# Attention scores as plain fp32 products over each head's own 64 rows, instead of split one-pass products

## The chip, the cores and the metric

The kernel runs on one core of a Trainium2 chip. The core has five engines that run side by side: TensorE (matrix products, PE in the profile; its weight loads are PEld), VectorE (DVE), ScalarE (ACT), GpSimd (POOL) and SyncE (SP), which here issues all DMA transfers in order. SBUF is the working memory of 128 partitions (rows); PSUM is the memory of 8 banks into which TensorE writes. The metric is device microseconds of one execution, lower is better.

## The reference

Softcapped attention for 4 batches of 12 heads, 448 positions, 64 features a head, followed by a bilinear feed-forward layer over the 1792 tokens of 768 features:

```
scores = cap * tanh((q @ k.T) / sqrt(64) / cap)       # [4, 12, 448, 448]
attn   = exp(scores - max); attn /= sum(attn) + 1e-9
x      = (attn @ v), heads side by side               # [1792, 768]
out    = ((x @ w_a) * (x @ w_b)) @ w_out              # w_a, w_b: [768, 1536], w_out: [1536, 768]
```

q and k are fp32 normal numbers with a spread of about 0.41; cap is 30. The outputs are fp32.

## The kernel before

**Pairs.** Heads are handled two at a time, 24 pairs in all. Each pair has 128 rows in SBUF: head A's 64 features on partitions 0 to 63, head B's on 64 to 127. The number 448 is cut into three chunks of 128 keys and a remainder of 64.

**The steps of a pair.** `load_pair` issues the loads of k, q and v. `prep_pair` brings q and k into the layout [feature, position] and makes the operands of the scores. `scores(pi, 0)` does chunks 0 and 1, `scores(pi, 1)` chunk 2 and the remainder: products into the PSUM tile `psc` (two banks, one for each head; two such tiles in turn), tanh on ScalarE out of `psc` (L270), exp in place (L271). The remainder of both heads shares one bank. GpSimd and VectorE add up the exponentials (L275 to L281, tile `psum`). `attend` multiplies with v (L293, L295, tile `pv`; plain fp32 products, each head in its own half of the columns), `normalize` sums over rows with small products (L308), takes reciprocals (L316), sends them through DRAM to broadcast them (L317, L321), and multiplies (L322). For pairs 0 to 11 the result is split into a high and a low part, `xhi` and `xlo` (L331, L332); for pairs 12 to 23 it goes to DRAM and is loaded later (L326, L337).

**How products are made.** `F32R` is a form of fp32 that TensorE multiplies in one pass with fewer bits. Where full precision is wanted in one-pass products, an operand is split into `hi` (the value cast to F32R) and `lo` (the rest), and a product is hi·hi + lo·hi + hi·lo. An operand of plain type F32 makes a plain fp32 product.

**q and k before.** For pairs 0 to 12, q and k are loaded as [112, 4, 2, 64], transposed by TensorE against the identity (L232, tiles `ptk`, `ptq`, `pt`) into PSUM, and read from there. For pairs 13 to 23 (`BLOCKED`) they are loaded in blocks of 32 features (L206, 128-byte pieces) and transposed by VectorE in 32x32 blocks (L223). Then ScalarE casts q's high part onto the head's own 64 rows of `qhh` (L238), and a copy of it goes onto the other 64 rows (L240 for pairs 0 and 1, a DMA at L242 after that); VectorE casts k's high part onto the own rows of `keys` (L245), and k's low part goes onto the other rows (L247, VectorE or GpSimd); GpSimd keeps the remainder's high parts on the diagonal of `kdiag` (L248); VectorE makes `qlo` (L250). So a product over all 128 rows is (k hi + k lo)·q hi of one head (L263), and one over the own 64 rows adds k hi·q lo (L264). The remainder takes three products over 128 rows (L268 twice, L269).

**Order.** A loop over pairs calls the steps in the order of a string, "PASNFTF" up to pair 12 and "SFANPFTF" after: P prepares the next pair, A and N attend and normalize the one before, S and T are the two halves of the scores, F runs a slice of the feed-forward generator `ffn`. A scheduler then orders each engine's instructions by that priority and by when it expects operands. `load_pair` runs two pairs ahead; q, k and their prepared tiles have two buffers, v three.

**The feed-forward part** is done in two groups of 896 tokens. Group 0 runs in slices between pairs 13 to 23 and finishes after them; group 1 follows. `ffn` makes products over 768 features (L429 to L431, tiles `pha`, `phb`), multiplies the halves (L434 to L438) and calls `ffn_out`, products with w_out (L460 to L462, tile `po`), added up in `acc` (L466). The weights come as 64-bit words and are converted by `ready_w` on ScalarE, VectorE and GpSimd (L389 to L394), written to DRAM for group 1 (L395), and split by `split_w` (L411, L412); the first loads are issued after pair 10's scores.

Of the kernel before, what the change touches and what calls it, by code (L numbers as in the profile page):

```python
# [9 lines left out]
F32 = mybir.dt.float32  # L10
# [11 lines left out]
def wide_cap_path(tc, q, k, v, wd, capt, ident, out):  # L22
    """The whole computation with the softmax's running maximum, for caps that exp alone can't span."""
# [93 lines left out]
def kernel(  # L117
# [30 lines left out]
    MAIN = NC3 * P  # L148
    R = S - MAIN
# [6 lines left out]
    BLOCKED = NPG + 1  # L156
# [21 lines left out]
    def f32(ap):  # L178
        return ap.bitcast(F32)
# [3 lines left out]
    # Keys of a pair side by side, R columns of zeros between them: the windows [A's last R | 0] and  # L183
    # [0 | B's first R] put both heads' remainders in one bank; kdiag has their high parts on its diagonal.
    koff, krem = (0, S + R), (MAIN, S + R)
    keys = [const.tile([P, 2 * S + R], F32R, tag=f"keys{i}", name=f"keys{i}") for i in range(2)]
    kdiag = [const.tile([P, P], F32R, tag=f"kdiag{i}", name=f"kdiag{i}") for i in range(2)]
# [4 lines left out]
    un = lambda ap: ap.rearrange("d (p c) -> d c p", c=NCH)  # L192
    pm = lambda ap: ap.rearrange("d (c p) -> d c p", c=NCH)
    sides = ((slice(0, D), slice(D, P)), (slice(D, P), slice(0, D)))
    raw, stk, prob, pvs = {}, {}, {}, {}

    def load_pair(pi):
        b, hp = divmod(pi, NP)
        for nm, src in (("k", k), ("q", q)):
            if pi >= BLOCKED:  # L200
                t = ld.tile([P, S // BLK, BLK], F32, tag=f"ld{nm}", name=f"ld{nm}_{pi}")
                for j in range(2):
                    for h in range(D // BLK):
                        rows = slice(j * D + h * BLK, j * D + (h + 1) * BLK)
                        cols = src[b, 2 * hp + j, :, h * BLK : (h + 1) * BLK]
                        nc.sync.dma_start(t[rows], cols.rearrange("(c p) d -> p c d", p=BLK))  # L206
                raw[nm, pi] = t
# [6 lines left out]
        nc.sync.dma_start(t, v[b, 2 * hp : 2 * hp + 2].rearrange("j s d -> (j s) d").rearrange("(c p) d -> p c d", p=P))  # L214
        raw["v", pi] = t

    def prep_pair(pi):
        tk, tq = raw.pop(("k", pi)), raw.pop(("q", pi))
        blocked = pi >= BLOCKED
        if blocked:  # L220
            pk, pq = (qk.tile([P, S], F32, tag=f"t{nm}", name=f"t{nm}_{pi}", bufs=1) for nm in "kq")
            for p_, t in ((pk, tk), (pq, tq)):
                nc.vector.transpose(p_, t.rearrange("p c d -> p (c d)"))  # L223
        else:
            if pi >= NPG:
                both = ps_sc.tile([P, 2, 512], F32, tag="pssc", name=f"pt_{pi}")
                pk, pq = both[:, 0], both[:, 1]
            else:
                pk, pq = (ps_1.tile([P, 512], F32, tag="ps1", name=f"pt{nm}_{pi}") for nm in "kq")
            for p_, t in ((pk, tk), (pq, tq)):  # L230
                for c in range(NCH):
                    nc.tensor.transpose(p_[:, c * CP : (c + 1) * CP], t[:, c].rearrange("p j d -> p (j d)"), ident[:CP, :CP])  # L232
        khl, kdg = keys[pi % 2], kdiag[pi % 2]
        qhh = qk.tile([P, 2, S], F32R, tag="qhh", name=f"qhh_{pi}")
        qlo = qk.tile([P, S], F32R, tag="qlo", name=f"qlo_{pi}")
        to, fr = (lambda x: x, lambda x: x) if blocked else (un, pm)
        for j, (own, oth) in enumerate(sides):
            nc.scalar.copy(to(qhh[own, j]), fr(pq[own, :S]))  # L238
            if pi < 2:
                nc.vector.tensor_copy(un(qhh[oth, j]), pm(pq[own, :S]))  # L240
            else:
                nc.sync.dma_start(f32(qhh[oth, j]), f32(qhh[own, j]))  # L242
        for j, (own, oth) in enumerate(sides):
            kj = khl[:, koff[j] : koff[j] + S]
            nc.vector.tensor_copy(to(kj[own]), fr(pk[own, :S]))  # L245
            eng = nc.gpsimd if blocked else nc.vector
            eng.tensor_sub(to(kj[oth]), fr(pk[own, :S]), to(f32(kj[own])))  # L247
            nc.gpsimd.tensor_copy(kdg[own, j * R : (j + 1) * R], f32(khl[own, krem[j] : krem[j] + R]))  # L248
        for j, (own, oth) in enumerate(sides):
            nc.vector.tensor_sub(to(qlo[own]), fr(pq[own, :S]), to(f32(qhh[own, j])))  # L250
        stk[pi] = (khl, kdg, qhh, qlo)

    def scores(pi, hf):
        khl, kdg, qhh, qlo = stk[pi]
        pf = pp.tile([P, 4 - hf, S], F32, tag=f"pf{hf}", name=f"pf_{pi}_{hf}")
        for i in range(2):
            c = 2 * hf + i
            n = 2 if c < NC3 else 1
            psc = ps_sc.tile([P, 2, 512], F32, tag="pssc", name=f"psc_{pi}_{c}")
            if n == 2:  # L260
                for j, (own, _) in enumerate(sides):
                    kc = khl[:, koff[j] + j * R + c * P : koff[j] + j * R + (c + 1) * P]
                    nc.tensor.matmul(psc[:, j, :S], kc, qhh[:, j], start=True, stop=False)  # L263
                    nc.tensor.matmul(psc[:, j, :S], kc[own], qlo[own], start=False, stop=True)  # L264
            else:
                for j in range(2):
                    kc = khl[:, MAIN + j * R : MAIN + j * R + P]
                    nc.tensor.matmul(psc[:, 0, :S], kc, qhh[:, j], start=(j == 0), stop=False)  # L268
                nc.tensor.matmul(psc[:, 0, :S], kdg, qlo, start=False, stop=True)  # L269
            nc.scalar.activation(pf[:, 2 * i : 2 * i + n], psc[:, :n, :S], AF.Tanh, scale=capt[:, 1:2])  # L270
# [5 lines left out]
        else:  # L276
            for j, (own, _) in enumerate(sides):
                nc.vector.scalar_tensor_tensor(  # L278
                    t[own, j], pf[own, 2], capt[own, 2:3], t[own, j], op0=ALU.add, op1=ALU.add
                )  # L280
            nc.gpsimd.tensor_add(t, t, pf[:, 0:2])  # L281

    def attend(pi):
# [10 lines left out]
        for j, (own, _) in enumerate(sides):  # L294
            nc.tensor.matmul(t[own, :S], tv[own, NC3], prob[pi, 1][own, 2], start=False, stop=True)  # L295
        del prob[pi, 0], prob[pi, 1]

    def normalize(pi):
# [20 lines left out]
        for j, (own, _) in enumerate(sides):  # L319
            row = rd[pi][j * NCH : (j + 1) * NCH].rearrange("(o c) p -> o (c p)", o=1)  # L320
            nc.sync.dma_start(den[own], row.to_broadcast([D, S]))  # L321
# [151 lines left out]
    with ExitStack():  # L473
# [100 lines left out]
```

## Time and profile before

| | us |
|---|---|
| three runs | 838.63, 844.20, 840.54 |
| median | 840.54 |
| span of the profiled execution | 838.4 |
| busy in the span: TensorE | 797.7 (95%) |
| weight load | 617.3 (74%) |
| VectorE | 545.9 (65%) |
| ScalarE | 367.1 (44%) |
| GpSimd | 342.6 (41%) |

The span runs from the first to the last instruction of the profiled execution; the page gives no other time for that execution, so the span is what the parts of the profile add up to, and the median of the timed runs lies 2.1 us above it. A group's row gives line, engine, operation, output<-inputs, shapes and count, then busy time and the mean ns of one, then the engine's idle time just ahead and what ended it. A timeline row gives start, length, engine and what ran; matmuls are pipelined, so their durations overlap and the distance between starts tells more. A wait's row gives the total time, how often, and the longest.

### The profile page before, as it was taken

To read this page: it belongs to the slowest core of one execution; us is meant where nothing else is said; L and a number is where in the kernel's file an instruction comes from. 1 tells how busy PE (TensorE), PEld (TensorE's weight loads), DVE (VectorE), ACT (ScalarE), POOL (GpSimd) and SP (SyncE) were. 2 spreads that over 40 slices of the span, in tenths; PEclk is the share of its full clock that TensorE was granted. 3 is DMA by queue.
4 is the path that set the end of the run, shared out by engine and by line. 5 is a ranking of instruction groups with operands and counts; after the bars stand their busy time and mean duration, and the time that the engine had idled before them with its cause. 6 is when DMAs were issued, how large, how long until landed. Compare 5 with 4: busy or idle time off the path is not lost. (4 is left out here: it accounts for less than half of the span.)

```text
span 838.4 us, 10618 instructions
## 1 busy us (share of the span) xinstructions
PE 797.7 (95%) x3968; PEld 617.3 (74%) x3968; DVE 545.9 (65%) x670; ACT 367.1 (44%) x450; POOL 342.6 (41%) x224
## 2 busy tenths in 40 slices
PE   5999999899699889989989999999999999999997
PEld 3444443566478668758758767989999999999996
DVE  6788998979947986796696688285224343343514
ACT  4788886565654543553654463212331121212110
POOL 1366665777655653674564363211112020202000
PEclk9999999699799999999999999999999999999999
DMA  6244447766662653553543342454111111111003
GB/s 130 67 115 113 112 110 165 165 168 178 193 176 84 198 167 87 172 158 105 170 152 101 121 165 84 136 186 150 57 57 57 57 56 57 40 56 57 1 1 134
DMA packets 131320, 95.54 MB, mean 114 GB/s; under 512 B 91200, under 2 KB 118848, under 8 KB 131264
## 3 DMA queue, kind: packets, MB, share of 16 engines
q1 hardware_dynamic: 131264, 94.81, 39.5%
q8 instruction: 33, 0.54, 0.3%
q14 instruction: 23, 0.19, 0.1%
HBM read 67.24 MB, written 22.50 MB: 107 GB/s over the span
## 5 line engine op out<-in xcount | busy, mean ns | idle before, releaser
L460 PE MATMUL po<-who,gh 128*128 128x384 f32 x336 | 116.5, 350 | 8.3 <-DVE acc L466 6.1
L461 PE MATMUL po<-wlo,gh 128*128 128x384 f32 x336 | 115.1, 343 | 4.9 <-DVE wlo L412 4.9
L462 PE MATMUL po<-who,gl 128*128 128x384 f32 x336 | 111.6, 341 | 1.0 <-DVE gl L438 1.0
L429 PE MATMUL pha<-xhi,wha 128*128 128x448 f32 x288 | 107.6, 374 | 1.4 <-DVE xhi L331 1.4
L429 PE MATMUL phb<-xhi,whb 128*128 128x448 f32 x288 | 107.2, 372 | 0.0
L430 PE MATMUL pha<-xlo,wha 128*128 128x448 f32 x288 | 106.3, 369 | 0.0
L430 PE MATMUL phb<-xlo,whb 128*128 128x448 f32 x288 | 105.9, 368 | 0.0
L431 PE MATMUL pha<-xhi,wla 128*128 128x448 f32 x288 | 105.8, 369 | 0.0
L431 PE MATMUL phb<-xhi,wlb 128*128 128x448 f32 x288 | 105.8, 368 | 0.0
L270 ACT ACTIVATE pf<-psc,capt 128x896 f32<-128x896 f32 x96 | 85.0, 912 | 40.4 <-PE psc L264 38.6
L466 DVE TENSOR_TENSOR acc<-po,acc 128x384 f32<-128x384 f32 x140 | 74.5, 551 | 32.0 <-PE po L462 31.8
L412 POOL TENSOR_TENSOR wlb<-wrb,whb 128x768 fp32r<-128x768 f32 x12 | 22.2, 1848 | 154.9 <-PE pha L431 106.3
L271 ACT ACTIVATE pf<-pf,capt 128x1792 f32<-128x1792 f32 (+1 forms) x48 | 77.0, 1603 | 1.0
L460 PEld LDWEIGHTS po<-who,gh 128*128 128x128 f32 x336 | 64.5, 192 | 16.0 <-DVE acc L466 8.4
L436 DVE TENSOR_TENSOR asb<-phb,asb 128x448 f32<-128x448 f32 x48 | 29.7, 619 | 69.3 <-PE phb L431 69.3
L263 PE MATMUL psc<-qhh,keys 128*128 128x448 f32 x144 | 67.1, 467 | 4.5 <-DVE qhh L240 2.9
L434 ACT COPY asb<-pha 128x448 f32<-128x448 f32 x48 | 25.5, 530 | 104.0 <-PE pha L431 99.2
L293 PE MATMUL pv<-pf,ldv 128*64 128x448 f32 x288 | 68.2, 593 | 2.2 <-ACT pf L271 2.2
L281 POOL TENSOR_TENSOR psum<-psum,pf 128x896 f32<-128x896 f32 x24 | 52.3, 2180 | 43.7 <-DVE psum L278 28.5
L264 PE MATMUL psc<-qlo,keys 64*128 64x448 f32 x144 | 69.1, 482 | 0.5 <-DVE qlo L250 0.5
L461 PEld LDWEIGHTS po<-wlo,gh 128*128 128x128 f32 x336 | 64.6, 192 | 6.6 <-DVE wlo L412 6.0
L438 DVE TENSOR_TENSOR gl<-asb,gh 128x448 fp32r<-128x448 f32 x48 | 54.5, 1136 | 20.8 <-ACT gh L437 20.7
(103 smaller groups left out, 1459.6 us busy)
## 6 DMA issues: line engine op xcount, KB each, us to landing
w64a<-in_moe_w_a_dram SPq DMA_DIRECT2D x12, 768.0 KB
w64b<-in_moe_w_b_dram SPq DMA_DIRECT2D x12, 768.0 KB
w64o<-in_moe_w_out_dram SPq DMA_DIRECT2D x12, 768.0 KB
ldv<-in_v_dram SPq DMA_DIRECT2D x24, 224.0 KB
den<-rd SPq DMA_DIRECT2D x48, 112.0 KB
out_dram<-acc SPq DMA_DIRECT2D x13, 384.0 KB
qhh<-qhh SPq DMA_DIRECT2D x44, 112.0 KB
wda<-wta SPq DMA_DIRECT2D x12, 384.0 KB
```

What stands on the lines that cost most here:

```text
L263: nc.tensor.matmul(psc[:, j, :S], kc, qhh[:, j], start=True, stop=False)
L264: nc.tensor.matmul(psc[:, j, :S], kc[own], qlo[own], start=False, stop=True)
L270: nc.scalar.activation(pf[:, 2 * i : 2 * i + n], psc[:, :n, :S], AF.Tanh, scale=capt[:, 1:2])
L271: nc.scalar.activation(pf, pf, AF.Exp, scale=capt[:, 0:1])
L293: nc.tensor.matmul(t[j * D : (j + 1) * D, :S], tv[:, j * (NC3 + 1) + c], p, start=(c == 0), stop=False)
L429: nc.tensor.matmul(t[:, :S], wh[:, kk], xhi[:, kk, cs], start=(kk == 0), stop=False)
L430: nc.tensor.matmul(t[:, :S], wh[:, kk], xlo[:, kk, cs], start=False, stop=False)
L431: nc.tensor.matmul(t[:, :S], wl[:, kk], xhi[:, kk, cs], start=False, stop=(kk == NK - 1))
L460: nc.tensor.matmul(t[:, :HALF], gh[:, cs], wh, start=(f == fs[0]), stop=False)
L461: nc.tensor.matmul(t[:, :HALF], gh[:, cs], wl, start=False, stop=False)
L462: nc.tensor.matmul(t[:, :HALF], gl[:, cs], wh, start=False, stop=(f == fs[-1]))
L466: nc.vector.tensor_add(acc[:, ti, hs], t[:, :HALF], acc[:, ti, hs])
```

## The change

All pairs now load q and k in blocks of 32 features and transpose them on VectorE, into the plain fp32 tiles `tk` and `tq` (two buffers each). The TensorE transposes, the split of q and k, the tiles `keys`, `kdiag`, `qhh`, `qlo`, and the copies that filled them are gone. A chunk's scores are one plain fp32 product for each head, over the head's own 64 rows: `tk[o, chunk]` by `tq[o]`, into that head's bank. The remainder is a product of 64 rows by 64 columns for each head, into its own half of the partitions of one bank. Positions are now in natural order for all pairs; the keys that head A has as its remainder are its last 64, head B's are its first 64, as before.

```diff
     def load_pair(pi):
         b, hp = divmod(pi, NP)
         for nm, src in (("k", k), ("q", q)):
-            if pi >= BLOCKED:
-                (the blocked load below)
-                continue
-            t = ld.tile([CP, NCH, 2, D], F32, tag=f"ld{nm}", name=f"ld{nm}_{pi}")
+            t = ld.tile([P, S // BLK, BLK], F32, tag=f"ld{nm}", name=f"ld{nm}_{pi}")
             for j in range(2):
-                nc.sync.dma_start(t[:, :, j, :], src[b, 2 * hp + j].rearrange("(p c) d -> p c d", c=NCH))
+                for h in range(D // BLK):
+                    rows = slice(j * D + h * BLK, j * D + (h + 1) * BLK)
+                    cols = src[b, 2 * hp + j, :, h * BLK : (h + 1) * BLK]
+                    nc.sync.dma_start(t[rows], cols.rearrange("(c p) d -> p c d", p=BLK))
             raw[nm, pi] = t
...
     def prep_pair(pi):
-        (transposes on TensorE or VectorE; qhh, keys, kdiag, qlo)
-        stk[pi] = (khl, kdg, qhh, qlo)
+        stk[pi] = []
+        for nm in "kq":
+            t = raw.pop((nm, pi))
+            tt = qk.tile([P, S], F32, tag=f"t{nm}", name=f"t{nm}_{pi}")
+            nc.vector.transpose(tt, t.rearrange("p c d -> p (c d)"))
+            stk[pi].append(tt)
 
     def scores(pi, hf):
-        khl, kdg, qhh, qlo = stk[pi]
+        tk, tq = stk[pi]
...
             psc = ps_sc.tile([P, 2, 512], F32, tag="pssc", name=f"psc_{pi}_{c}")
-            if n == 2:
-                for j, (own, _) in enumerate(sides):
-                    kc = khl[:, koff[j] + j * R + c * P : koff[j] + j * R + (c + 1) * P]
-                    nc.tensor.matmul(psc[:, j, :S], kc, qhh[:, j], start=True, stop=False)
-                    nc.tensor.matmul(psc[:, j, :S], kc[own], qlo[own], start=False, stop=True)
-            else:
-                for j in range(2):
-                    kc = khl[:, MAIN + j * R : MAIN + j * R + P]
-                    nc.tensor.matmul(psc[:, 0, :S], kc, qhh[:, j], start=(j == 0), stop=False)
-                nc.tensor.matmul(psc[:, 0, :S], kdg, qlo, start=False, stop=True)
+            for j, o in enumerate(own):
+                at = j * R + c * P if n == 2 else krem[j]
+                to = psc[:, j, :S] if n == 2 else psc[o, 0, :S]
+                nc.tensor.matmul(to, tk[o, at : at + (P if n == 2 else R)], tq[o], start=True, stop=True)
...
     with ExitStack():
-        for i in range(2):
-            nc.gpsimd.tensor_scalar_mul(keys[i][:, S : S + R], ident[:, :R], 0.0)
-            nc.gpsimd.tensor_scalar_mul(kdiag[i], ident, 0.0)
```

Here `own` is the pair of slices (rows 0 to 63, rows 64 to 127) and `krem` is (448 - 64, 0). The rest of the diff renames loop variables.

More of the change, by code (lines that the diff above doesn't have):

```diff
@@ L147 @@
     NC3 = S // P
-    MAIN = NC3 * P
-    R = S - MAIN
+    R = S - NC3 * P
     PFB = 2
@@ L155 @@
     BLK = 32
-    BLOCKED = NPG + 1
     dr = ctx.enter_context(tc.tile_pool(name="dr", bufs=1, space=bass.MemoryType.DRAM))
@@ L182 @@
     psum = [const.tile([P, 2, S], F32, tag=f"psum{i}", name=f"psum{i}") for i in range(2)]
-    koff, krem = (0, S + R), (MAIN, S + R)
-    keys = [const.tile([P, 2 * S + R], F32R, tag=f"keys{i}", name=f"keys{i}") for i in range(2)]
-    kdiag = [const.tile([P, P], F32R, tag=f"kdiag{i}", name=f"kdiag{i}") for i in range(2)]
     xhi = const.tile([P, NK, GT], F32R, tag="xhi", name="xhi")
@@ L190 @@
     acc = const.tile([P, NTI, DM], F32, tag="acc", name="acc")
-    un = lambda ap: ap.rearrange("d (p c) -> d c p", c=NCH)
-    pm = lambda ap: ap.rearrange("d (c p) -> d c p", c=NCH)
-    sides = ((slice(0, D), slice(D, P)), (slice(D, P), slice(0, D)))
+    own, krem = (slice(0, D), slice(D, P)), (S - R, 0)
     raw, stk, prob, pvs = {}, {}, {}, {}
@@ L199, in load_pair @@
         for nm, src in (("k", k), ("q", q)):
-            if pi >= BLOCKED:
-                t = ld.tile([P, S // BLK, BLK], F32, tag=f"ld{nm}", name=f"ld{nm}_{pi}")
-                for j in range(2):
[L203 to L207, printed above, removed]
-                continue
-            t = ld.tile([CP, NCH, 2, D], F32, tag=f"ld{nm}", name=f"ld{nm}_{pi}")
+            t = ld.tile([P, S // BLK, BLK], F32, tag=f"ld{nm}", name=f"ld{nm}_{pi}")
             for j in range(2):
-                nc.sync.dma_start(t[:, :, j, :], src[b, 2 * hp + j].rearrange("(p c) d -> p c d", c=NCH))
+                for h in range(D // BLK):
+                    rows = slice(j * D + h * BLK, j * D + (h + 1) * BLK)
+                    cols = src[b, 2 * hp + j, :, h * BLK : (h + 1) * BLK]
+                    nc.sync.dma_start(t[rows], cols.rearrange("(c p) d -> p c d", p=BLK))
             raw[nm, pi] = t
@@ L217, in prep_pair @@
     def prep_pair(pi):
[L218 to L223, printed above, removed]
-        else:
[L225 to L250, printed above, removed]
@@ L259, in scores @@
             psc = ps_sc.tile([P, 2, 512], F32, tag="pssc", name=f"psc_{pi}_{c}")
-            if n == 2:
-                for j, (own, _) in enumerate(sides):
-                    kc = khl[:, koff[j] + j * R + c * P : koff[j] + j * R + (c + 1) * P]
[L263 to L266, printed above, removed]
-                    kc = khl[:, MAIN + j * R : MAIN + j * R + P]
-                    nc.tensor.matmul(psc[:, 0, :S], kc, qhh[:, j], start=(j == 0), stop=False)
-                nc.tensor.matmul(psc[:, 0, :S], kdg, qlo, start=False, stop=True)
+            for j, o in enumerate(own):
+                at = j * R + c * P if n == 2 else krem[j]
+                to = psc[:, j, :S] if n == 2 else psc[o, 0, :S]
+                nc.tensor.matmul(to, tk[o, at : at + (P if n == 2 else R)], tq[o], start=True, stop=True)
             nc.scalar.activation(pf[:, 2 * i : 2 * i + n], psc[:, :n, :S], AF.Tanh, scale=capt[:, 1:2])
@@ L276, in scores @@
         else:
[L277 to L280, printed above, removed]
+            for j, o in enumerate(own):
+                nc.vector.scalar_tensor_tensor(t[o, j], pf[o, 2], capt[o, 2:3], t[o, j], op0=ALU.add, op1=ALU.add)
             nc.gpsimd.tensor_add(t, t, pf[:, 0:2])
@@ L293, in attend @@
                 nc.tensor.matmul(t[j * D : (j + 1) * D, :S], tv[:, j * (NC3 + 1) + c], p, start=(c == 0), stop=False)
-        for j, (own, _) in enumerate(sides):
-            nc.tensor.matmul(t[own, :S], tv[own, NC3], prob[pi, 1][own, 2], start=False, stop=True)
+        for o in own:
+            nc.tensor.matmul(t[o, :S], tv[o, NC3], prob[pi, 1][o, 2], start=False, stop=True)
         del prob[pi, 0], prob[pi, 1]
@@ L318, in normalize @@
         den = sm.tile([P, S], F32, tag="den", name=f"den_{pi}")
-        for j, (own, _) in enumerate(sides):
+        for j, o in enumerate(own):
             row = rd[pi][j * NCH : (j + 1) * NCH].rearrange("(o c) p -> o (c p)", o=1)
-            nc.sync.dma_start(den[own], row.to_broadcast([D, S]))
+            nc.sync.dma_start(den[o], row.to_broadcast([D, S]))
         nc.vector.tensor_mul(den, t[:, :S], den)
```

## Prediction

> **What bounds the kernel now.** I read the span first, then the table of stretches, then TensorE's timeline inside a stretch, then the groups by shape, the queue's issues and the waits.
>
> ```profile
> span 838.4 us, 10618 instructions
> ```
> ```profile
> 80.00:100.00 20.00, 20.00 (x110) 9.38 (x110) 18.12 (x22) 16.53 (x17) 12.36 (x10) 1.00 0.46 112
> 140.00:160.00 20.00, 17.79 (x58) 8.15 (x55) 19.77 (x19) 14.57 (x18) 14.50 (x11) 0.67 0.93 197
> 200.00:220.00 20.00, 14.70 (x72) 10.07 (x73) 18.05 (x17) 14.14 (x18) 13.48 (x6) 0.84 0.64 198
> 600.00:700.00 100.00, 100.00 (x528) 95.34 (x527) 36.17 (x52) 21.97 (x39) 15.40 (x9) 1.00 0.17 52
> ```
>
> The columns of the second block are the stretch, its length, then busy time (and instructions) of TensorE, its weight load, VectorE, ScalarE and GpSimd, the granted clock, the DMA share and GB/s. The span has four parts: a start; stage A, the attention of the first pairs alone, where TensorE is busy 20.00 of 20 us at full clock; stage B, attention and the first half of the feed-forward part together, where VectorE is at times nearly full (18 to 20 of 20 us) and TensorE now and then stops and loses clock; and stage C, the second half alone, where TensorE is full again (600 to 700 above). The change touches nothing in C. So TensorE is the bound, and the question is what one pair's scores cost it. One period of stage A on TensorE:
>
> ```profile
> 97.07 0.45 PE L263 MATMUL psc<-qhh,keys 128*128 128x448 f32 x1
> 97.45 0.47 PE L264 MATMUL psc<-qlo,keys 64*128 64x448 f32 x1
> ...
> 100.25 2.48 PE L293 MATMUL pv<-pf,ldv 128*64 128x448 f32 x12
> 102.65 0.97 PE L295 MATMUL pv<-pf,ldv 64*64 64x448 f32 x4
> 103.55 0.47 PE L263 MATMUL psc<-qhh,keys 128*128 128x448 f32 x1
> ...
> 105.95 0.59 PE L308 MATMUL sum<-psum,sel 128*32 128x112 f32 x16
> 106.47 0.60 PE L232 MATMUL ptk<-ident,ldk 112*128 112x112 f32 x4
> ...
> 107.23 0.45 PE L263 MATMUL psc<-qhh,keys 128*128 128x448 f32 x1
> ```
> ```profile
> 180.45 0.36 PE L429 MATMUL phb<-xhi,whb 128*128 128x448 f32 x1
> ...
> 182.49 0.36 PE L430 MATMUL phb<-xlo,whb 128*128 128x448 f32 x1
> ```
>
> Read the starts, not the durations, which overlap. A pair takes 107.23 - 97.07 = 10.16 us: scores of the first two chunks 3.18 (eight one-pass products, 0.40 each), the product with v 3.30, the other two chunks 2.40, sums 0.52, transposes 0.76. In the feed-forward part products of the same 448 columns start 2.04 us / 10 = 0.204 us apart. So in the scores, where a 128-row product and a 64-row product alternate, each pays some 0.2 us more than its streaming: the price of changing the shape of the array's tile.
>
> **What the change costs and saves.** *The fp32 product.* The trace has no fp32 product of 64 rows by 128 columns; the nearest rows are those of the product with v. L293's twelve instructions are six fp32 products, so one product is two instructions. They start over 102.65 - 100.25 = 2.40 us, 0.20 each, and their loads show how:
>
> ```profile
> 60.37 0.14 PEld L293 LDWEIGHTS pv<-pf,ldv 128*64 128x64 f32 x2 [0.23 <-issue]
> 60.74 0.14 PEld L293 LDWEIGHTS pv<-pf,ldv 128*64 128x64 f32 x2 [0.23 <-issue]
> ```
>
> Two loads, one for each head's half of the columns, come every 0.37 us, the time of two passes (2 x 0.19). So one instruction lasts two passes, and the two heads run side by side in different column halves. An fp32 product thus costs 1.5/2 = 0.75 us when two share the array, for both, and 0.75 us each when they don't. Whether heads in different *row* halves (0-63 and 64-127, all 128 columns, a bank of PSUM each) share it like column halves, no row shows. Bounds for one chunk of both heads: 0.75 side by side, 1.50 one after the other, and 4 x (0.375 + 0.20) = 2.3 if each instruction also pays the change of shape that L263 and L264 pay. I take 0.75, since the nearest fp32 rows, whose operands also come in two disjoint parts, run side by side: L295's 64-row products are the only ones on separate row halves, and their four instructions take 103.55 - 102.65 = 0.90 us, not 1.5.
>
> The last chunk writes both heads into one bank, from separate row halves. On the page "TensorEngine Tiling (Array Packing)" the Trainium skill, in "Gotcha 1: PSUM Pressure", says that different row tiles cannot access the same PSUM bank at once. L295's two heads do just that in 0.90 us, so the trace disagrees, and I keep 0.90 for this chunk. For two 64-row tiles of 128 columns the same page's "Key Properties" lets them load and multiply in parallel; by it the sum is the one below. No run here shows that yet.
>
> *Stage A.* Scores in a row: first half 2 x 0.75 + one change of shape 0.2 = 1.7 us; second half 0.2 + 0.75 + 0.90 = 1.85. Together 3.55 instead of 5.58. Transposes (0.76) leave TensorE. So 10.16 - 2.03 - 0.76 = 7.4 us a pair. What is late next:
>
> ```profile
> L245 DVE CAST keys<-tk 64x448 fp32r<-64x448 f32 x22 | 16.7, 759 | 3.9 <-PE psc L268 3.5
> L250 DVE TENSOR_TENSOR qlo<-tq,qhh 64x448 fp32r<-64x448 f32 x22 | 24.3, 1103 | 0.4
> L223 DVE STREAM_TRANSPOSE tk<-ldk 128x448 f32<-128x448 f32 x11 | 7.0, 632 | 0.1
> L238 ACT CAST qhh<-ptq 64x448 fp32r<-64x448 f32 x24 | 22.7, 944 | 8.6 <-PE ptq L232 6.5 <-DVE qhh L240 1.9
> ```
> ```profile
> L206 SPq DMA_DIRECT2D ldk<-in_k_dram x44: 311/478/2137, 117.3 to 372.0; - x44
> L321 SPq DMA_DIRECT2D den<-rd x48: 459/584/1452, 38.7 to 533.2; - x48
> L214 SPq DMA_DIRECT2D ldv<-in_v_dram x24: 368/385/1322, 3.5 to 440.2; - x24
> L317 SPq DMA_DIRECT2D rd<-rec x24: 584/608/667, 36.6 to 531.0; - x24
> ```
>
> ScalarE: 16.53 us in 20, or 8.4 a pair, less two casts of 0.94 = 6.5. VectorE: 18.12 in 20, or 9.2 a pair; the six casts and differences of about 0.95 go, two transposes of 0.63 come: about 4.7. GpSimd loses its diagonal copies. The DMA queue (SP): eight loads of 0.48, v 0.39, the reciprocals 0.61, two broadcasts of 0.58 = 6.0 us a pair; the two copies of q's high part go. DMA engines: 0.46 of 10.16 = 4.7 us a pair, of which q and k are, by the bytes that the program moves (448 of 1120 KB), 1.9; if pieces half as long doubled that, 5.7 after the copies of q's high part (224 KB, 0.9) are gone. All are below 7.4, ScalarE, the queue and the DMA engines not by much. I take **7.6 a pair**, between 7.4 and 8.2 (the queue's 6.0 with the 2 us between reciprocal and broadcast unfilled). Pairs 2 to 10, from 36.05 to 129.22 us (rows below), are nine periods: 9 x 2.56 = **-23** (-18 to -25).
>
> *Start.*
>
> ```profile
> 10.24 1.11 PE L263 MATMUL psc<-qhh,keys 128*128 128x448 f32 x2 [2.86 <-DVE qhh L240]
> ...
> 20.49 0.74 PE L264 MATMUL psc<-qlo,keys 64*128 64x448 f32 x1
> ...
> 36.05 0.45 PE L263 MATMUL psc<-qhh,keys 128*128 128x448 f32 x1
> ...
> 129.22 0.45 PE L263 MATMUL psc<-qhh,keys 128*128 128x448 f32 x1
> ...
> 157.45 0.74 PE L429 MATMUL pha<-xhi,wha 128*128 128x448 f32 x1
> ```
>
> Eight loads at 0.48 from 0.7 us and about 3 us of landing and one transpose give a first score at about 8.5 us, not 10.24, though there are twice as many loads ahead of it. Then two pairs' scores and one product with v: 2 x 3.55 + 3.3 + 0.5 = 11 us; at the start products take 0.74 and stand 0.67 apart instead of 0.40, so I give the first half of it twice its time, 16 or 17 us; now it is 36.05 - 10.24 = 25.8. Estimate **-10** (-5 to -13). Work between 129.22 and the first feed-forward product at 157.45: two pairs' worth, but the first weights must be converted by then: **-5** (0 to -9).
>
> *Stage B.* There, scores stand single between feed-forward products:
>
> ```profile
> 165.02 0.37 PE L263 MATMUL psc<-qhh,keys 128*128 128x448 f32 x1
> ...
> 166.51 0.47 PE L431 MATMUL pha<-xhi,wla 128*128 128x448 f32 x1
> ...
> 512.31 0.57 PE L268 MATMUL psc<-qhh,keys 128*128 128x448 f32 x2
> ...
> 512.91 0.34 PE L460 MATMUL po<-who,gh 128*128 128x384 f32 x1
> ...
> 514.05 0.97 PE L293 MATMUL pv<-pf,ldv 128*64 128x448 f32 x4
> 514.96 0.45 PE L460 MATMUL po<-who,gh 128*128 128x384 f32 x1
> ```
>
> A chunk is 1.49 + 0.1 = 1.6 us now, the last 0.60 (it has the feed-forward products' shape, so no change): 3 x 1.6 + 0.6 = 5.4 a pair. Four fp32 instructions between such products take 0.91 + 0.1 = 1.0: 4.0 after. Eleven pairs x 1.4 = **-15** (-11 to -22, the latter if chunks stand together as in stage A). VectorE loses 41 us in B (L245 and L250 above), GpSimd and ScalarE their part of the splitting. TensorE's longest stops there:
>
> ```profile
> PE po L461 <- DVE wlo L412: 4.9, 3, 2.3
> PE po L460 <- DVE acc L466: 4.9, 3, 2.4
> PE psc L268 <- ACT pf L270: 4.8, 1, 4.8
> ```
>
> They are 14.6 us, and the clock of 0.67 and 0.84 in two stretches above costs 20 x 0.33 + 20 x 0.16 = 9.8 more. VectorE has less to do, but B is shorter too, so its share hardly changes: **-5** (-20, most of these 24, to +10, if the weights' conversions fall behind a faster TensorE).
>
> Sum: -10 - 23 - 5 - 15 - 5 = -58, 838.4 - 58 = 780. The profiled execution has no time of its own beside its span; the three runs' median is 840.54, 2 us above, so **782**. Its own bounds, adding the ends: 749 to 816.
>
> **Rivals.** *One after the other* (0.10): the row halves don't share. A chunk is then 1.5: A 5.8 instead of 5.58, but the transposes go, so -5; start -5; B 3 x 1.75 + 1.0 = 6.25, so +9; stalls -5. Sum -6: **834**. Against it speak L295's 0.90 us. *A drain at every instruction* (0.07, the slower side): row halves change the tile as L263 and L264 do; 2.3 a chunk, 3 x 2.3 + 0.95 + 0.2 = 8.05 a pair in A, 2.47 more less 0.76: +15 for nine pairs, +5 around 129-157, B 3 x 2.4 + 1.0 = 8.2, so +31, stalls -5: **886**. For it: each of those alternations costs 0.40; against: there one tile contains the other, here they are disjoint. It decides as soon as a chunk takes over 1.8 us. *The DMA queue becomes stage A's bound* (0.09): with the weights loading, four loads took 4.96 us,
>
> ```profile
> 137.05 4.96 SPq L206 DMA_DIRECT2D ldq<-in_q_dram  x4
> ```
>
> and at even 0.9 each the queue needs 7.2 + 2.2 = 9.4 with unfilled waits 10: A and the transition gain nothing, start -5, B -15, stalls -5: **815**. *Last chunk alone serial* (0.03): +0.75 x 24 = +18: **800**.
>
> **How the numbers follow.** The forecast as summed has 0.71; within it I give 757 to 805 most of the weight. The range 757 to 835 takes in the queue's case and the serial one, leaving the drain and tails of some 0.12 out. A change under 1%, 8 us here, can't be told from none in runs that spread from 838.63 to 844.2. Faster by over 1%: forecast, queue, last chunk: 0.83. Within: the serial case, 0.10. Slower: the drain, 0.07.
>
> **What would show it.** Score instructions of two heads starting in twos, each pair of instructions 0.37 us after the last; a period of 7.4 to 7.8 us in stage A with TensorE still full and ScalarE at some 85%; scores as single groups of about 1.0 us in B; the first score near 8.5 us; C as long as before. The prediction is wrong if score instructions start singly at 0.375 us or more, if ScalarE or VectorE waits on q and k loads in A, or if TensorE's stops in B grow because the conversions of the weights no longer keep up.

## The result, and the profile after

The changed kernel took **802.10 us** (median of four runs, 801.45 to 807.11), the kernel before 842.37 us (four runs, 838.63 to 844.45): a ratio of 0.954, with a 95% interval of 0.951 to 0.958. The forecast was 782, within 757 to 835. The profiled execution took 802.73 us, with a span of 800.9 us; so 37.5 us of the span went (838.4 before), not 58. One execution among all that follow, of the kernel before with less conversion, took 859.46 us at a granted clock of 0.846 and is left out of the figures below.

The head of the changed kernel's profile page:

```profile
span 800.9 us, 10115 instructions
PE 743.4 (93%) x3888; PEld 562.4 (70%) x3888; DVE 434.6 (54%) x570; ACT 330.8 (41%) x402; POOL 283.2 (35%) x150
```

VectorE lost 111 us of busy time (545.9 before), GpSimd 59, TensorE 54. Its table of stretches (columns as before the change: stretch, length, busy time and instructions of TensorE, its weight load, VectorE, ScalarE and GpSimd, granted clock, DMA share, GB/s):

```profile
80.00:100.00 20.00, 19.59 (x132) 6.20 (x130) 10.10 (x18) 17.39 (x17) 12.80 (x8) 1.00 0.60 121
140.00:160.00 20.00, 14.17 (x60) 10.52 (x59) 15.03 (x15) 11.71 (x14) 11.24 (x6) 0.83 0.46 158
600.00:700.00 100.00, 100.00 (x524) 94.97 (x523) 42.40 (x63) 17.24 (x27) 16.60 (x9) 1.00 0.18 56
```

In stage A TensorE is nearly full as before, VectorE has fallen to half, and ScalarE stands at 17.39 of 20, 87% where some 85% was forecast. In stage B TensorE's stops and the low clock (0.83 in 140:160) are still there. TensorE's timeline shows the start, one period of stage A, and scores within stage B:

```profile
7.29 5.75 PE L222 MATMUL psc<-tq,tk 64*128 64x448 f32 x16 [7.29 <-DVE tq L209]
...
26.52 1.77 PE L222 MATMUL psc<-tq,tk 64*128 64x448 f32 x8
...
35.69 0.95 PE L259 MATMUL sum<-psum,sel 128*32 128x112 f32 x16 [3.74 <-POOL psum L232]
...
47.03 1.77 PE L222 MATMUL psc<-tq,tk 64*128 64x448 f32 x8
48.74 0.97 PE L244 MATMUL pv<-pf,ldv 128*64 128x448 f32 x4
...
50.54 1.02 PE L222 MATMUL psc<-tq,tk 64*128 64x448 f32 x4
51.49 0.59 PE L259 MATMUL sum<-psum,sel 128*32 128x112 f32 x16
52.01 0.97 PE L222 MATMUL psc<-tq,tk 64*64 64x448 f32 x4
52.91 1.72 PE L244 MATMUL pv<-pf,ldv 128*64 128x448 f32 x8
54.57 1.77 PE L222 MATMUL psc<-tq,tk 64*128 64x448 f32 x8
...
101.07 1.77 PE L222 MATMUL psc<-tq,tk 64*128 64x448 f32 x8
...
123.06 0.47 PE L380 MATMUL pha<-xhi,wha 128*128 128x448 f32 x1
...
128.15 1.77 PE L222 MATMUL psc<-tq,tk 64*128 64x448 f32 x8
129.86 0.47 PE L380 MATMUL pha<-xhi,wha 128*128 128x448 f32 x1
...
156.54 0.97 PE L222 MATMUL psc<-tq,tk 64*64 64x448 f32 x4
157.44 0.47 PE L381 MATMUL pha<-xlo,wha 128*128 128x448 f32 x1
```

Read starts. Two chunks of both heads, eight instructions, take 48.74 - 47.03 = 1.71 us in stage A and 129.86 - 128.15 = 1.71 in stage B; the third chunk 51.49 - 50.54 = 0.95, the remainder 52.91 - 52.01 = 0.90. That undisturbed period is 54.57 - 47.03 = 7.54 us, with 1.71 + 0.95 + 0.90 = 3.56 of scores; the prediction had 7.4 and 3.55. The loads come in twos:

```profile
47.03 0.30 PEld L222 LDWEIGHTS psc<-tq,tk 64*128 64x128 f32 x4 [0.70 <-issue]
47.52 0.19 PEld L222 LDWEIGHTS psc<-tq,tk 64*128 64x128 f32 x2 [0.18 <-issue]
47.89 0.19 PEld L222 LDWEIGHTS psc<-tq,tk 64*128 64x128 f32 x2 [0.18 <-issue]
```

Two loads every 0.37 us, as the forecast had it for heads that share the array; which head a load belongs to, the trace does not say. For the gain by stage, these are the marks of the traces (us): the first score; the first and third reciprocal and the tenth (pairs 0, 2, 9); the first feed-forward product; the first reload of a stored pair (`xl`), where stage B ends; the end of the last product.

| | first score | pair 0 | pair 2 | pair 9 | first feed-forward | B ends | last product |
|---|---|---|---|---|---|---|---|
| before | 10.2 | 35.4 | 55.8 | 127.0 | 157.5 | 545.6 | 832.3 |
| after | 7.3 | 21.6 | 44.6 | 99.7 | 123.1 | 506.4 | 795.0 |
| difference | -2.9 | -13.8 | -11.2 | -27.3 | -34.4 | -39.2 | -37.3 |

Each mark is that of one execution: two runs below that begin as the kernel before does (new scores for pairs 13 to 23 only; before with less conversion) had pair 0's reciprocal at 32.9 and 32.8, so some 2.5 us of a difference can lie in the execution. Nearly all of the gain is there before the first feed-forward product; stage B became only 4.7 us shorter (388.1 to 383.4), and C is 1.8 longer. Two things stay open after this: whether the sharing is what made A shorter, and where stage B's share went. TensorE's waits, first up to 110 us, then from 110 to 530 us (columns: total, how often, longest), are the first clue:

```profile
PE sum L259 <- POOL psum L232: 7.8, 5, 3.7
```
```profile
PE po L411 <- DVE acc L417: 7.8, 7, 3.4
PE pha L380 <- DVE xhi L282: 5.8, 1, 5.8
PE po L412 <- DVE wlo L363: 5.8, 1, 5.8
```

### The profile page after: what moved, and what is told of

It is laid out like the page before. It is cut to its first block, busy times and chain, and to the rows that moved or that the text cites. A ratio compares the mean times of both kernels' runs of the same rounds, so it can differ in the third digit from the quotient of the medians.

```text
span 800.9 us, 10115 instructions
## 1 busy us (share of the span) xinstructions
PE 743.4 (93%) x3888; PEld 562.4 (70%) x3888; DVE 434.6 (54%) x570; ACT 330.8 (41%) x402; POOL 283.2 (35%) x150
## 5 line engine op out<-in xcount | busy, mean ns | idle before, releaser
L222 PE MATMUL psc<-tq,tk 64*128 64x448 f32 (+1 forms) x384 | 96.6, 591 | 11.1 <-DVE tq L209 7.3
L232 POOL TENSOR_TENSOR psum<-psum,pf 128x896 f32<-128x896 f32 x24 | 54.0, 2248 | 91.1 <-DVE psum L231 81.7
L222 PEld LDWEIGHTS psc<-tq,tk 64*128 64x128 f32 (+1 forms) x384 | 29.7, 178 | 53.5 <-issue 27.9
L413 PEld LDWEIGHTS po<-who,gl 128*128 128x128 f32 x336 | 64.2, 192 | 4.1 <-DVE gl L389 3.4
```

Source lines behind the costliest of these rows:

```text
L222: nc.tensor.matmul(to, tk[o, at : at + (P if n == 2 else R)], tq[o], start=True, stop=True)
L413: nc.tensor.matmul(t[:, :HALF], gl[:, cs], wh, start=False, stop=(f == fs[-1]))
```

## The experiments

Times on different chips are compared through the ratio to the kernel before on the same chip.

### Two parts of the change alone

**The new scores for pairs 0 to 12 only**, the old split scores for the rest (all pairs with the blocked load, the rest split as before):

```diff
-    BLOCKED = NPG + 1
+    BLOCKED = 0
...
+        if pi <= NPG:
+            stk[pi] = (pk, pq)
+            return
...
+            if pi <= NPG:
+                (scores as after the change)
```

> All pairs load in blocks and transpose on VectorE; pairs 0 to 12 use the plain fp32 scores, pairs 13 to 23 the split ones as before. First feed-forward product at 123 us as in the changed kernel (157 before). Theory A, stage B's gain was lost to VectorE, which can't feed a faster TensorE there: B as long as before or longer by a few us, 805 to 812 us. Theory B, the stops of stage B come from its earlier start, when the weights' first conversions and x are not ready: B is longer by their cost, some 10 us, 816 to 820.

Measured: 815.83 us (813.54 to 817.59), ratio 0.970 (0.966 to 0.975). The period between pairs 2 and 9 was 7.97 us, the first feed-forward product at 130.9, stage B 390.0 long. B's length, 1.9 more than before, is theory A's, the time nearer theory B's: the first feed-forward product came 7.8 us later than in the changed kernel, which neither theory had (TensorE stopped 5.4 us for one of GpSimd's sums at 112 us). So the run doesn't decide between them.

**The new scores for pairs 13 to 23 only**, pairs 0 to 12 as before:

```diff
+            if pi >= BLOCKED:
+                (scores as after the change)
```

> Pairs 0 to 12 as before (TensorE transposes, split scores), pairs 13 to 23 with the plain fp32 scores. First feed-forward product at 157 us as before. Theory A (VectorE can't feed a faster TensorE in stage B): B 383 instead of 388 us, so 836 to 839. Theory B (the stops come from the earlier start alone): the score products' 14 us and some of the stalls come off: 822 to 829.

Measured: 825.77 us (823.66 to 829.58), ratio 0.983 (0.979 to 0.988), period 10.17 as before. That is theory B's range. The two halves are worth 24.5 and 14.5 us, together 39, the whole of the change: they neither help nor hinder each other much. But the late half's 14.5 isn't all stage B's: its first feed-forward product came at 148.9 (8.6 earlier than before, where the theories had it unmoved) and B took 380.0, 8.1 less.

**The transposes alone**: all pairs loaded in blocks and transposed on VectorE, scores and splitting as before.

```diff
-    BLOCKED = NPG + 1
+    BLOCKED = 0
```

> The kernel before with all pairs loaded in blocks and transposed on VectorE, and everything else of the split kept. Theory: TensorE loses 0.76 of 10.16 us a pair in stage A and sets the pace still, 9.4 us: nine periods give 7 us, 833 to 837 in all. Rival 1: VectorE or ScalarE, with two transposes more, become the bound of stage A: 842 or more. Rival 2: the start's long chain shortens as well: 828 to 832.

Measured: 842.39 us (838.69 to 846.75), ratio 1.001 (0.998 to 1.005): no change. TensorE's timeline of that kernel:

```profile
65.09 0.47 PE L263 MATMUL psc<-qhh,keys 128*128 128x448 f32 x1
...
74.44 0.47 PE L263 MATMUL psc<-qhh,keys 128*128 128x448 f32 x1
...
84.66 0.59 PE L308 MATMUL sum<-psum,sel 128*32 128x112 f32 x16 [2.96 <-POOL psum L281]
85.18 3.17 PE L293 MATMUL pv<-pf,ldv 128*64 128x448 f32 x8
```

This period is 74.44 - 65.09 = 9.35 us, 0.8 less than 10.16, as the 0.76 of transposes say. But the products with v of pairs 2 and 10 stand 85.7 us apart, 10.7 a pair, against 79.9 before. One loss is the stop of 2.96 us for GpSimd's sum: behind it eight products take 3.10 us (85.18 to the next start, 88.28) that take 1.65 elsewhere, at a granted clock of 0.50. GpSimd's sums make only 3.3 us of waits up to 150 us, though. The larger sign is VectorE, with two transposes more a pair (columns as above):

```profile
100.00:120.00 20.00, 19.40 (x98) 8.11 (x96) 19.48 (x20) 15.84 (x17) 16.25 (x13) 1.00 0.53 105
```

It is busy 19.48 of 20 us here and 79.26 of those 85.7, or 9.9 a pair, more than TensorE's 9.35; and its reciprocals fall behind the row sums, from 1.7 us for pair 2 to 5.4 for pair 9, so that from reciprocal to reciprocal a period is 11.8. So the first rival came, with its engine and its number (842 or more); no run here takes VectorE's work away to prove it. (In this kernel `tk` and `tq` have one buffer each, in the changed one two.) Alone, this part of the change is worth nothing.

### Is it the row halves?

**Both heads from the same rows.** This takes away the disjoint rows and leaves number, shape, banks and order of the products.

```diff
-                nc.tensor.matmul(to, tk[o, ...], tq[o], start=True, stop=True)
+                r = own[0] if n == 2 else o
+                nc.tensor.matmul(to, tk[r, ...], tq[r], start=True, stop=True)
```

> The changed kernel with both heads' products of the three 128-key chunks taken from rows 0 to 63 (so head B gets head A's scores there; the number, shape and order of the instructions stay). Theory: the two products share the array only because they lie in different row halves. In one half they follow each other: 1.5 us a chunk instead of 0.75, 2.25 us more a pair, a period of 9.8 to 10.1 us in stage A instead of 7.87, 845 to 858 us in all. Rival: what made the scores cheaper is only that shapes no longer alternate, and nothing is shared: 800 to 804. Second rival: without a change of half the weight loads no longer hide either, 0.2 us more for each instruction: 1.45 us more a chunk, 890 to 910.

Measured: 826.70 us (822.27 to 827.47), ratio 0.982 (0.977 to 0.987). One period of stage A on its TensorE:

```profile
59.53 3.27 PE L223 MATMUL psc<-tq,tk 64*128 64x448 f32 x8
62.73 0.97 PE L245 MATMUL pv<-pf,ldv 128*64 128x448 f32 x4
...
64.53 1.77 PE L223 MATMUL psc<-tq,tk 64*128 64x448 f32 x4
66.23 0.59 PE L260 MATMUL sum<-psum,sel 128*32 128x112 f32 x16
...
69.31 2.90 PE L223 MATMUL psc<-tq,tk 64*128 64x448 f32 x7
```

Eight instructions take 62.73 - 59.53 = 3.20 us instead of 1.71, four 1.70 instead of 0.95; the period is 69.31 - 59.53 = 9.78. With 0.2 us for the change of shape that is 1.5 us a chunk, the prediction's bound "one after the other", so the sharing is the row halves' doing: it is shown. It also answers what made A shorter: without the sharing the period is 9.78 us again, where it was 10.16 before the change. On the whole, though, this kernel was faster than the 845 to 858 us that I expected: stage B, with 22 us more of scores, was 3.6 us longer than after. That is taken up below.

**Another order of the eight instructions.** I first thought that the sharing hangs on the order head A, head B, A, B: one instruction after another is started, so two of one head in a row should leave the other half idle. The edit issues head A's two chunks, then head B's:

```diff
+            pscs = [ps_sc.tile(...) for c in range(2)]
+            for j, o in enumerate(own):
+                for c in range(2):
+                    nc.tensor.matmul(pscs[c][:, j, :S], tk[o, ...], tq[o], start=True, stop=True)
```

> The changed kernel, but in the first half of a pair's scores the four products are issued head A chunk 0, head A chunk 1, head B chunk 0, head B chunk 1, instead of the heads in turn. Theory: two products share the array only where neighbours in the order lie in different row halves. Then eight instructions fill about seven places of 0.375 us instead of four: 2.8 us instead of 1.70 for two chunks, 1.1 us more for each of 24 pairs where TensorE sets the pace, 816 to 828 us in all (802 for the changed kernel). Rival: the queue picks any instruction whose row half is free, so order doesn't matter: 1.70 us and 802. Second rival: the gain is the missing change of shape, not sharing: 3.0 us in both kernels, 802.

Measured: 802.53 us, ratio 0.957 (0.952 to 0.961). It told nothing: the scheduler put the heads back in turn for every pair but the first. The same edit with the order of the four products held:

> As the run with the heads apart, but the four products of the first two chunks are pinned in the order A chunk 0, A chunk 1, B chunk 0, B chunk 1 (in the earlier run the scheduler put them back in turn for all pairs but the first). Theory: only neighbours in the order share the array: seven places of 0.375 us instead of four, 2.8 us instead of 1.70 for two chunks; with 1.1 us for 24 pairs 816 to 828 us. Rival: TensorE takes any instruction whose row half is free: 1.70 us and 802.

Measured: 805.29 us (803.87 to 809.34), ratio 0.959 (0.954 to 0.964), where my theory had 816 to 828. Its timeline:

```profile
47.44 1.78 PE L221 MATMUL psc<-tq,tk 64*128 64x448 f32 x8
49.15 0.97 PE L253 MATMUL pv<-pf,ldv 128*64 128x448 f32 x4
```

1.71 us, as with the heads in turn. The theory fell: with four products standing A, A, B, B in the program, eight instructions take no longer. Since those of one row half follow each other (3.20 us), B's must have run beside A's, if the order of the program held on the chip; the trace doesn't show which head a record belongs to.

### Where did stage B's gain go?

I added up TensorE's rows between the first feed-forward product and the first reload: for each kind of product the time from one start to the next, idle time apart. Scores in B fell from 56.7 to 42.5 us, 14.2 less; the forecast said 15. But idle stops rose from 20.6 to 26.4, the product with v and the sums together took 2.1 more, the products with w_out 1.4 more. So the price of a score was right, and most of the time came back as waiting. The longest stop is at 148 us, TensorE's row and then VectorE's rows ahead of it:

```profile
148.30 0.74 PE L380 MATMUL pha<-xhi,wha 128*128 128x448 f32 x1 [5.83 <-DVE xhi L282]
```
```profile
131.21 0.85 DVE L267 RECIPROCAL rec<-sum 128x112 f32<-128x112 f32 x1
...
135.06 2.73 DVE L343 SCALAR_TENSOR_TENSOR wtb<-w64b,wtb 128x768 int32<-128x768 int32 x1
137.91 2.40 DVE L344 SCALAR_TENSOR_TENSOR wtb<-wsb,wtb 128x768 f32<-128x768 bf16 x1
140.23 0.55 DVE L342 TENSOR_SCALAR wta<-w64a 128x768 int32<-128x768 int32 x1
140.82 2.48 DVE L343 SCALAR_TENSOR_TENSOR wta<-w64a,wta 128x768 int32<-128x768 int32 x1
143.41 2.64 DVE L344 SCALAR_TENSOR_TENSOR wta<-wsa,wta 128x768 f32<-128x768 bf16 x1
145.97 0.61 DVE L273 TENSOR_TENSOR den<-pv,den 128x448 f32<-128x448 f32 x1
146.62 1.63 DVE L282 CAST xhi<-den 128x448 fp32r<-128x448 f32 x1
```

The last pair of group 0, pair 11, has its reciprocal at 131.21; its result is multiplied and cast only at 145.97 and 146.62, behind five steps of two weights' conversions. TensorE idles 5.83 us. Two more things lengthen this chain: the broadcasts of that reciprocal (L272) were issued by the queue only at 137.30 and 138.45, after its store at 132.57, and four of the five steps took 2.40 to 2.73 us where the same steps take 0.95 at other times (the last section says beside what), some 6.4 us together, more than the stop.

**Less conversion, after and before.** Two of VectorE's three conversion steps for each block of weights are left out, about 94 us of VectorE's work in B (L343 and L344); the transfers and the rest stay.

```diff
-        nc.vector.scalar_tensor_tensor(wt, hw, -0x40000000, wt, op0=ALU.bitwise_and, op1=ALU.bitwise_or)
-        nc.vector.scalar_tensor_tensor(f32(wt), ab, MIN_NORMAL_HI, f32(wt), op0=ALU.is_ge, op1=ALU.mult)
```

In the changed kernel:

> The changed kernel without two of VectorE's three steps in each weight's conversion (the sign and top bit, and the flush of small values), so the weights and the output are other numbers; all transfers and products stay. Some 95 us less VectorE work before stage C. Theory (VectorE makes stage B's stops): stops from 26 to under 10 us and half clock from 27 to under 12 us: 778 to 787. Rival (DMA or the order of the queue makes them): 796 to 803.

Measured: 779.82 us (779.06 to 780.95), ratio 0.928 (0.924 to 0.932), the theory's range. In the kernel before:

> The kernel before without the same two VectorE steps of each weight's conversion (so other weights and another output). It tells whether VectorE took the gain from the change or from both kernels alike. Theory: VectorE's conversions cost the changed kernel more, since it needs the weights sooner: the kernel before gains 8 to 14 us, 827 to 833, and the two relieved kernels stand 48 us or more apart, near the forecast 58. Rival: the conversions stop both alike: 817 to 821, 38 to 41 us apart, and the missing gain of stage B has another cause.

Measured: 817.14 us (816.71 to 818.27), ratio 0.974 (0.968 to 0.981), the rival's range. TensorE's longest waits in the changed kernel with less conversion, from 110 to 500 us:

```profile
PE psc L222 <- ACT pf L223: 3.8, 1, 3.8
PE po L411 <- DVE gl L387: 3.4, 3, 1.7
PE pha L378 <- DVE xhi L282: 2.7, 1, 2.7
```

The stop for `wlo` is gone, the one for `xhi` fell from 5.8 to 2.7 us, and all stops in B from 26.4 to 10.1. So the conversions make most of stage B's stops; but they do so in both kernels, and the two steps cost both the same by the ratios: 0.954 - 0.928 = 0.026 after, 1 - 0.974 = 0.026 before, 22 us of 840. The change itself is worth 0.974 - 0.928 = 0.046 of the time without them and 1 - 0.954 = 0.046 with them: so in the whole time the conversions did not eat more of the changed kernel's gain, to within some 7 us, by the intervals of the ratios. In B they did: there the change is worth 4.7 us with them and 11.0 without, and ahead of B 34.4 with them and 28.4 without. The windows of stage B (last two columns of busy time: ScalarE, GpSimd), one fence a kernel: before, after, both heads from the same rows, before with less conversion, after with less conversion.

```profile
157.50:545.60 388.10, 367.48 (x1802) 280.62 (x1799) 292.68 (x325) 196.46 (x248) 218.30 (x127) 0.96 0.48 144
```
```profile
123.10:506.40 383.30, 356.92 (x1816) 260.83 (x1813) 251.92 (x286) 189.60 (x233) 173.58 (x86) 0.96 0.47 142
```
```profile
139.80:526.80 387.00, 375.13 (x1817) 270.89 (x1814) 250.34 (x287) 190.84 (x233) 173.83 (x86) 0.98 0.47 140
```
```profile
150.30:522.80 372.50, 363.92 (x1802) 278.13 (x1799) 203.61 (x256) 197.53 (x251) 204.56 (x127) 0.98 0.51 153
```
```profile
121.90:483.40 361.50, 351.36 (x1816) 257.21 (x1813) 166.59 (x218) 188.75 (x233) 166.59 (x86) 0.99 0.50 152
```

| stage B, us | scores | stops | at half clock | length | first conversion on VectorE to the end of B |
|---|---|---|---|---|---|
| before | 56.7 | 20.6 | 28.7 | 388.1 | 406.1 |
| after | 42.5 | 26.4 | 27.3 | 383.4 | 398.2 |
| new early pairs only | 56.0 | 24.9 | 30.6 | 390.0 | 408.1 |
| new late pairs only | 43.3 | 21.2 | 23.9 | 380.0 | 392.2 |
| same rows | 65.0 | 11.9 | 12.7 | 387.0 | 401.8 |
| before, less conversion | 57.2 | 8.6 | 17.1 | 372.5 | 385.5 |
| after, less conversion | 41.7 | 10.1 | 6.8 | 361.5 | 372.7 |

(The time at half clock lies within the other columns and isn't added to them.) With the conversions whole, 22.5 us more of scores ("after" to "same rows") lengthen B by 3.6: the stops take 14.5 less. The other way, 14.2 us less ("before" to "after") shorten it by 4.7, 13.5 less ("new early pairs only" to "after") by 6.6, 13.4 less ("before" to "new late pairs only") by 8.1. With less conversion 15.5 us less of scores shorten B by 11.0. So in B a good part of the scores fills time that TensorE would otherwise wait in, and a cheaper score in part buys waiting. That the weights' conversions hold B up is shown by the two runs with less of them; which link of that chain sets the pace is not shown. VectorE is busy only 251.92 of 383.30 us there, so it is not full on the whole.

**The weights two pairs earlier**, to get the stop at 148 us out of the way:

```diff
-            if pi == NPG - 2:
+            if pi == NPG - 4:
                 load64()
                 load64()
-            if pi == NPG - 1:
+            if pi == NPG - 3:
                 ready_w()
```

> The changed kernel, with the first weights' loads, conversions and splits issued two pairs earlier (after pair 8's and 9's scores instead of 10's and 11's). Theory: stage B starts earlier now, and VectorE's queue is then full of the first weights' conversions, behind which the reciprocal and the product of pair 11 and the high part of x wait; two pairs earlier VectorE is half idle. The three stops in the first 65 us of B fall from 14 us to 6 or less: 792 to 797 us. Rival: the stops come from the DMA engines (128-byte pieces of q and k beside the weights), which are no less busy: 800 to 806.

Measured: 802.69 us (800.71 to 805.64), ratio 0.956 (0.951 to 0.961): nothing won. The stop went and B shrank to 371.9, but stage A had conversions in it now and its period rose to 10.0; the first feed-forward product came at 133.9 instead of 123.1, and B ended at 505.8 instead of 506.4. The boundary moved, the end of B did not. The time is the rival's, but its reason, the DMA engines, is not shown by it: the stop for `xhi` did go.

**One of group 0's conversions on another engine**: `lo` of w_out for group 0 on GpSimd instead of VectorE.

```diff
-        (nc.vector if nm == "o" else nc.gpsimd).tensor_sub(lo, wt, f32(hi))
+        (nc.vector if nm == "o" and g else nc.gpsimd).tensor_sub(lo, wt, f32(hi))
```

> The changed kernel with the low part of w_out's blocks made on GpSimd instead of VectorE in group 0 (12 operations of 1.4 us off VectorE). Theory: the stop of 5.8 us at 185 us, where the first products with w_out wait for that low part behind VectorE's queue, shrinks below 2 us and the clock drop after it goes: 793 to 799. Rival: GpSimd's queue is as late, and with two engines on SBUF each is slower: 802 to 806.

Measured: 802.07 us (800.45 to 804.91), ratio 0.957 (0.952 to 0.961), no change. The stop of 5.8 us for `wlo` went, and TensorE waited elsewhere: B was 382.2 long.

### GpSimd's sum in stage A

Most of the 7.8 us of waits for `psum` lies in the start: 2.09 and 3.74 us, ending at 20.90 and 35.69, and 1.15 at 106.75. Between pairs 2 and 9 it is 0.83 us; there the row sums come every 7.72 us and the reciprocals every 7.87, against 7.54 in the undisturbed period. Two edits, for pairs 0 to 11. The first of GpSimd's two sums on VectorE:

```diff
-            nc.gpsimd.tensor_add(t, pf[:, 0:2], pf[:, 2:4])
+            (nc.vector if pi < NPG else nc.gpsimd).tensor_add(t, pf[:, 0:2], pf[:, 2:4])
```

> The changed kernel with the first sum of exponentials of pairs 0 to 11 on VectorE instead of GpSimd. Theory: in stage A GpSimd's two sums (4.5 us a pair, one behind the other with VectorE's step between) come late for the row sums, 7.8 us of waits up to 110 us; with one gone the period is 7.5 instead of 7.9 and the start's two waits shrink: 794 to 799. Rival: VectorE's own queue then holds up the transposes or the reciprocals: 802 or more.

Measured: 803.71 us (802.17 to 809.45), ratio 0.958 (0.953 to 0.964), a miss: the period rose to 8.52, and the same wait grew:

```profile
PE sum L259 <- POOL psum L232: 13.4, 9, 5.4
```

The sum that TensorE waits for is the second one. So that one went to VectorE instead:

```diff
-            nc.gpsimd.tensor_add(t, t, pf[:, 0:2])
+            (nc.vector if pi < NPG else nc.gpsimd).tensor_add(t, t, pf[:, 0:2])
```

> The changed kernel with the second sum of exponentials (the last link before the row sums) of pairs 0 to 11 on VectorE instead of GpSimd; the earlier run had moved the first sum, which isn't last. Theory: the last link gets 1.2 us shorter, TensorE waits no more for GpSimd in stage A, the period is 7.5 instead of 7.87 and B begins 3 to 6 us earlier. If that is kept: 796 to 800. Rival: stage B gives it back, since VectorE's conversions, not TensorE, set when the first group ends (506 us after two other moves in stage A): 801 to 804.

Measured: 800.92 us (797.89 to 802.17), ratio 0.954 (0.950 to 0.959), between the theory's range and the rival's. The period fell to 7.67 from reciprocal to reciprocal and 7.53 from sum to sum, so the term exists, but the first feed-forward product came only 0.5 us earlier than after the change, and the ratio is the changed kernel's own. No version was clearly faster than the changed kernel, except the one that leaves conversion work out.

## Why the prediction was right, and where it was not

Of the 20.5 us that are missing (58 forecast, 37.5 measured), some 15 are stage B's, 4.4 stage A's and 1.8 stage C's.

**The shared row halves: right.** 0.75 us for a chunk of both heads was the term on which all hung, and the trace before could not show it. It measured 1.71 for two chunks with one change of shape (1.7 forecast); undone by one edit, 3.20. "One after the other" and "a drain at every instruction" are out, and with them the slower side. The Trainium skill, page "TensorEngine Tiling (Array Packing)", "Key Properties", lets different tiles load and multiply in parallel; the trace agrees, with two loads every 0.37 us.

**The last chunk: right.** 0.90 us for four instructions that write one bank from two row halves (52.01 to 52.91, and 156.54 to 157.44). The same page's "Gotcha 1: PSUM Pressure" would forbid that to be parallel; the measurement decides against it for products that also go to different partitions.

**Start: right.** By the forecast's own rows: pair 2's first score came at 26.52 instead of 36.05 us, -9.5 where -10 was forecast, and the very first at 7.29, not 8.5.

**Stage A: short.** The nine periods from there to pair 11's first score took 101.07 - 26.52 = 74.55 us instead of 93.17: -18.6, not -23, at the edge of the range (-18 to -25). (93.17 is 10.35 a period; the forecast took 10.16.) The first of the nine took 12.98 us: it holds the stop of 3.74 us for GpSimd's sum, and behind it eight products took 2.93 us (36.57 to 39.50) that take 1.65 at 45.38. The eight others took 7.70 each, where 7.6 was forecast. The list of what would be late next had ScalarE, VectorE, the queue and the DMA engines with figures, but for GpSimd only that it loses its copies; that was the gap. The rival of the DMA queue did not come: TensorE's waits up to 110 us name no load after the first (17.39 of 20 on ScalarE, 0.60 on the DMA engines in 80:100).

**Transition: right.** 123.06 - 101.07 = 21.99 us instead of 28.23: -6.2, forecast -5 (0 to -9).

**Stage B: the scores right, the sum wrong.** Scores -14.2, forecast -15. The step that failed is the next one: "VectorE has less to do, but B is shorter too, so its share hardly changes: -5". It treated stops as a term beside the scores, to be added. They are not independent: measured, stops went up by 5.8 and other products by 3.5 (2.1 and 1.4), and B gave 4.7 instead of 20. Of the signs named for a wrong prediction this one came in part: TensorE's stops in B grew. Had I asked of each microsecond of scores "what else would TensorE do here?", the view was there: TensorE stopping and losing clock in the same stretches in which VectorE was nearly full. The upper bound of the stall term (+10) covered it: -10 - 23 - 5 - 15 + 10 = -43, or 797, and with the 4.4 us missing in A and C's 1.8 that is near the measured time. That bound was drawn for conversions that fall behind a faster TensorE. That conversions stop B is shown; that they cost more after the change than before is seen in B alone, not in the whole time. (Its own bounds mix two starting points: from 840.5 the ends add up to 751 and 816, not 749 and 816.)

**Stage C:** +1.8, forecast 0.

## What to carry to other kernels

Two products with 64 rows each belong on the two row halves of the array, their operands in separate halves of SBUF's partitions: a plain fp32 product for two heads then cost 0.75 us a chunk, less than the 1.6 us of four one-pass products on split operands with their changes of shape, and the splitting's work on the other engines goes too. Ask of each stage, before a saving on the busiest engine is booked there, whether that engine also stops in it; where it does, take the saving and the stops as one term, since part of the saving can come back as waiting (here some 15 to 70% of a change in the scores showed in B's length). Test it in the cheapest way: make the engine's work dearer, and see whether the stage grows.

## What was not expected of the hardware

- **Order didn't matter for the sharing.** With the four products of two chunks in the order A, A, B, B, eight instructions took 1.71 us, as in turn; on the same rows 3.20. How TensorE brings them side by side stays open.
- **VectorE's conversions took 0.9 us or 2.3 to 2.8 us for the same work, by what GpSimd was doing when they began.** The step of L343 at 135.06, shown above with 2.73 us, stood beside this row:

```profile
134.61 2.37 POOL L232 TENSOR_TENSOR psum<-psum,pf 128x896 f32<-128x896 f32 x1 [1.35 <-DVE psum L231]
```

  Of all 36 steps of L343 ten took 2.27 to 2.78 us. In each of the ten a GpSimd instruction was already running when the step began, and the step ended 0.8 us after that instruction did (137.79 and 136.97 here). The other 26 took 0.89 to 0.96 us: in five of them a GpSimd instruction began while the step ran, in 21 none ran. So a step waited for a GpSimd instruction ahead of it, and not for one behind it. The Trainium skill, page "GPSIMD Engine Reference", "1. Specifications", has GpSimd share its way into SBUF with VectorE's instructions that read two SBUF inputs, which these do; the trace agrees. No run here took GpSimd away to test it, or to see how much of stage B's stops it makes.
- **Some of TensorE's stops cost more than themselves.** In the kernel with the transposes alone eight products took 3.10 us behind a stop of 2.96 us and 1.65 elsewhere. In stage B the changed kernel spent 27.3 us at half clock with 26.4 us of stops, against 6.8 with 10.1 with less conversion. Not every stop did it: the changed kernel's of 3.28 us that ended at 122.54 had a granted clock of 1.00 from 115 to 130 us.
